# V of the first block in token pairs: loads in runs of 512 bytes, scores in tiles of 64 rows by 32 columns, values in tiles of 32 rows by 64 columns

## The chip, the cores and the metric

The kernel runs on one core of one Trainium2 chip. The metric is the device time of one execution in microseconds (us). The kernel before took 278.22 us, the median of three runs (277.86 to 278.23).

## What is computed

Attention inside chunks of 64 tokens, followed by a feed-forward layer with a squared ReLU. Batch 8, 8 heads, 576 tokens, head dimension 64; the feed-forward layer has 4608 tokens, width 512 and 2048 hidden units.

```python
scores = scale * np.matmul(q_c, k_c.transpose(0, 1, 2, 4, 3))   # per chunk of 64 tokens
attn = np.exp(scores) / np.sum(np.exp(scores), axis=-1, keepdims=True)
out = np.matmul(attn, v_c)
x = out.transpose(0, 2, 1, 3).reshape(B * S, H * D)
h = np.maximum(x @ w_in, 0.0)
return h * h @ w_out
```

## The kernel before

The tokens are worked in nine blocks of 512 (two groups of 256 each). For a block the kernel computes attention, transposes the result `x` to `xT`, multiplies by `w_in` (`ffn_in`, matmuls at line L621, PSUM tiles `ps_ffn`), squares, and multiplies by `w_out` (L795 for the first block, L678 for the others). The order of all instructions is written out by hand, each engine works through its own in that order, and all loads are issued by SyncE's queue (SP), one after another. While PE runs one block's feed-forward layer, attention of the next block is put in between, and loads of later blocks are issued by slot.

The first block has no layer before it to hide behind, and has code of its own, which is what the change touches. It is worked in two halves `u` of four heads, each over 512 tokens (eight chunks):

- `load_half` (L238) loads Q and K of a half, four tokens a partition, so that one run is 1024 bytes. The order on SP is Q, K of half 0, Q, K of half 1, then V of both halves (`load_v_half`, L247, eight loads), then `load_w_in(0)` (L173), all of which are issued ahead of the rest of `w_in`, `w_out` and the loads of block 1.
- `w_in` and `w_out` are loaded in eight pieces of 512 KB each into five buffers `w_st`, and cast to bf16 by GpSimd (POOL, L176 and L184). Two of the 16 hidden tiles `ft` need one piece of `w_in`; the first piece is cast in two halves.
- `transpose_half` (L268, copies L277) transposes Q and K on PE. `keep_busy` (L337) puts matmuls with no use between, to fill PE.
- `scores_half` (L289) multiplies K and Q of each chunk and head on a tile of 64 by 64 of the PE array and takes the exponential `e` on ACT (L296).
- `values_half(e, x, u, j)` (L309) multiplies `e` by V for half of the chunks (`j`) of one half of the heads. V has a column of ones behind each head's 64 columns, so column 64 of the result is the sum of the exponentials. DVE takes its reciprocal (L316) and multiplies (L317). PSUM tiles `ps_att` have two buffers, which scores and values share.
- `transpose_x_half` (L325, copy L329) transposes a quarter of `x` and copies it into `xT`. Four calls make the whole `xT` of the first block.
- V of the first block lies in `v_first`, a view on the space of `w_sum`, so the profile calls it `w_sum`.

At the end of this front the code issues the first half of the contraction of `ft` 0 and 1 (`begun`, four L621 matmuls that need `xT` of heads half 0 alone), and then the whole stream of `ffn_in`.

Of the kernel before, what the change touches and what calls it, by code (L numbers as in the profile page):

```python
# [10 lines left out]
FP32 = mybir.dt.float32  # L11
# [6 lines left out]
def kernel(  # L18
# [9 lines left out]
    nc = tc.nc  # L28

    B, H, S, D = q.shape  # L30
# [49 lines left out]
    w_sum = w_pool.tile([128, 3, n_ft // 2, d_model // 2], BF16, name="w_sum")  # L80
# [57 lines left out]
    for g in range(n_grp):  # L138
        if is_whole(g):
# [3 lines left out]
            b, s = chunks[g][0]  # L143
# [68 lines left out]
    def transpose_qk(g, q_pool, k_pool):  # L212
# [13 lines left out]
            transpose_paired(g, which, bank)  # L226
            copy_paired(copy, qkT[:, which], bank)

    v_first = w_sum.rearrange("p i f c -> p (i f c)")[:, 0:8 * H * (D + 1)].bitcast(
        FP32).rearrange("p (t h d) -> p t h d", t=4, h=H)  # L230
    nc.gpsimd.memset(v_first[:, :, :, D:D + 1], 1.0)

    first = chunks[blocks[0][0]][0]

# [8 lines left out]

    def load_v_half(u):
        b, s = first
        for t in range(4):
            nc.sync.dma_start(  # L247
                out=v_first[:, t, 4 * u:4 * u + 4, 0:D],
                in_=v[b, 4 * u:4 * u + 4, s + 128 * t:s + 128 * t + 128, :].rearrange(
                    "h s d -> s h d"))  # L250

    def bank_bf16():
        return ps_ffn.tile([128, 512], FP32, name="ps_ffn").bitcast(BF16)
# [25 lines left out]
    def scores_half(qkT):  # L279
        qT, kT = (qkT[:, w].rearrange("c t h q -> c (t h q)").rearrange(  # L280
            "c (h n q) -> c h n q", h=2, n=8) for w in range(2))
        ps = ps_att.tile([128, 1024], FP32, name="ps_att")
        for h in range(2):
            for t in range(4):
                for a in range(2):
                    for p in range(2):
                        rows = slice(64 * a, 64 * a + 64)
                        o0 = a * 512 + h * 256 + t * 64
                        nc.tensor.matmul(  # L289
                            out=ps[64 * p:64 * p + 64, o0:o0 + 64],  # L290
                            lhsT=kT[rows, h, 2 * t + p],
                            rhs=qT[rows, h, 2 * t + p],
                            start=True, stop=True)
        e = att_pool.tile([128, 2, n_hp, 2, 64], BF16, name="e")
        flat = e.rearrange("p a h t q -> p (a h t q)")
        nc.scalar.activation(  # L296
            out=flat.rearrange("p (b q i) -> p b q i", q=16, i=4),
            in_=ps.rearrange("p (b i q) -> p b q i", i=4, q=16), func=AF.Exp, scale=scale)
        return flat.rearrange("p (a h t q) -> p a h t q", a=2, h=2, t=4)

    def values_half(e, x, u, j):
        v_bf = v_first.bitcast(BF16)
        ps = ps_att.tile([128, 2, 512], FP32, name="ps_att")
        for t in range(2):
            for h in range(2):
                for a in range(2):
                    for p in range(2):
                        o0 = (2 * t + h) * (D + 1)
                        nc.tensor.matmul(  # L309
                            out=ps[64 * p:64 * p + 64, a, o0:o0 + D + 1],  # L310
                            lhsT=e[64 * p:64 * p + 64, a, h, 2 * j + t, :],
                            rhs=v_bf[64 * p:64 * p + 64, 2 * j + t, 4 * u + 2 * h + a, 1::2],
                            start=True, stop=True)
        o = ps[:, :, 0:4 * (D + 1)].rearrange("p a (h d) -> p a h d", d=D + 1)
        rec = att_pool.tile([128, 2, n_hp], FP32, name="rec", bufs=4)
        nc.vector.reciprocal(out=rec, in_=o[:, :, :, D])  # L316
        nc.vector.tensor_tensor(  # L317
            out=x[:, 4 * j:4 * j + 4].rearrange("p b a d -> p a b d"),
            in0=o[:, :, :, 0:D],
            in1=rec.to_broadcast([128, 2, n_hp, D]),  # L320
            op=ALU.mult)

    def transpose_x_half(x, u, j, copy, psb):
        for b in range(4):
            nc.tensor.transpose(  # L325
                out=psb[:, b * 128:(b + 1) * 128],
                in_=x[:, 4 * j + b].rearrange("p a d -> p (a d)"),
                identity=ident)
        copy(  # L329
            out=xTs[0][:, 2 * j:2 * j + 2, 2 * u:2 * u + 2, :],  # L330
            in_=psb[:, 0:512].rearrange("p (t h q) -> p t h q", t=2, h=2))

    def keep_busy(n, ps=None):
        if ps is None:
            ps = ps_ffn.tile([128, 512], FP32, name="ps_ffn")
        for _ in range(n):
            nc.tensor.matmul(  # L337
                out=ps[:, 0:256], lhsT=ident, rhs=ident_f32.bitcast(BF16), start=True, stop=True)
# [496 lines left out]
    for u in range(2):  # L835
        load_v_half(u)
# [3 lines left out]
    xs = [att_pool.tile([128, 2, n_hp, 2, D], BF16, name="x", bufs=3).rearrange(  # L840
        "p t h a d -> p (t h) a d") for _ in range(2)]
# [4 lines left out]
    transpose_half(kh[0], qkTs[0][:, 1], [V, A], by_token=True)  # L846
    keep_busy(3)
    e0 = scores_half(qkTs[0])
    transpose_half(qh[1], qkTs[1][:, 0], [V])
    keep_busy(2)  # L850
    transpose_half(kh[1], qkTs[1][:, 1], [V, A], by_token=True)
    values_half(e0, xs[0], 0, 0)
    keep_busy(2)
    e1 = scores_half(qkTs[1])
    values_half(e0, xs[0], 0, 1)
    transpose_x_half(xs[0], 0, 0, A, bank_bf16())
    keep_busy(4)
    values_half(e1, xs[1], 1, 0)
    transpose_x_half(xs[0], 0, 1, A, bank_bf16())
    keep_busy(6)  # L860
    xb = [bank_bf16(), bank_bf16()]
    begun = {ft: ps_ffn.tile([128, 512], FP32, name="ps_ffn") for ft in range(2)}
    transpose_x_half(xs[1], 1, 0, A, xb[0])
    values_half(e1, xs[1], 1, 1)
    keep_busy(3, begun[0])
    transpose_x_half(xs[1], 1, 1, V, xb[1])
    for ft in range(2):
# [136 lines left out]
```

## Time and profile before

| | |
|---|---|
| median of three runs | 278.22 us |
| the profiled execution, device time | 277.18 us |
| its span in the profile | 275.4 us, 7355 instructions |
| PE busy | 267.3 us (97%), 3047 matmuls |
| DVE, ACT, POOL busy | 73%, 56%, 34% |
| main DMA queue (q1) | 135968 packets, 55.72 MB, 86.8% of the 16 engines' time |
| DMA queue of instructions (q8) | 24 packets, 0.39 MB |
| granted clock of PE | 1.00 throughout |

The page divides the span into 40 slices of 6.9 us and gives the busy share of each engine in tenths. PE is the engine for matmuls, PEld its weight loads, DVE VectorE, ACT ScalarE, POOL GpSimd, SPq the queue from which SyncE issues DMAs. A line as L621 is a line of the kernel. `out<-in` names the tiles that an instruction writes and reads; what stands in brackets behind a row is the idle time before it and what ended it. The chain of waits is followed back from the last instruction, at each step to what released it.

### The profile page before, as it was taken

How to read it: one execution, taken by the hardware profiler on the slowest of the kernel's cores; microseconds unless marked ns; L12 is line 12 of the kernel's file. 1: busy time of each engine (PE TensorE's matmuls, PEld its weight loads, DVE VectorE, ACT ScalarE, POOL GpSimd, SP SyncE). 2: the span in 40 equal slices, each digit the busy share in tenths (PEclk: the TensorE clock that was granted, in tenths of full speed). 3: DMA queues.
4: the chain of work that ended last, by engine and by line, in shares of the span. 5: the costliest groups of instructions: out<-in, count | busy, mean ns of one | idle time of the engine just before them, and what ended most of it. 6: DMA issues, size and time to landing. Idle time of an engine off the chain costs nothing.

```text
span 275.4 us, 7355 instructions
## 1 busy us (share of the span) xinstructions
PE 267.3 (97%) x3047; PEld 185.5 (67%) x3047; DVE 202.2 (73%) x313; ACT 155.5 (56%) x262; POOL 92.9 (34%) x106
## 2 busy tenths in 40 slices
PE   7889999999999999999999999999999999999994
PEld 4544454888775587658755875587658755875683
DVE  1546516689986997599769776977599769777793
ACT  1537605796347782768186918682768186317710
POOL 2037768140433800380029002900380029003412
PEclk9999999999999999999999999999999999999999
DMA  7999999999999999999999799858799981623004
GB/s 233 228 334 356 369 340 233 227 224 181 286 167 189 261 199 176 292 236 185 259 249 210 153 187 286 189 115 181 225 280 181 210 317 38 193 47 108 0 2 152
DMA packets 136417, 57.11 MB, mean 207 GB/s; under 512 B 110336, under 2 KB 130048, under 8 KB 136384
## 3 DMA queue, kind: packets, MB, share of 16 engines
q1 hardware_dynamic: 135968, 55.72, 86.8%
q0 software_dynamic: 272, 0.79, 0.7%
q8 instruction: 24, 0.39, 0.6%
q10 hardware_dynamic: 144, 0.13, 0.1%
q14 instruction: 9, 0.07, 0.1%
HBM read 36.70 MB, written 9.44 MB: 168 GB/s over the span
## 4 chain that ended last, share of the span: by engine, by line
PE 81%; DMA 9%; SPq 7%; POOL 1%; issue 1%; DVE 0%
PE ps_ffn L678 36%; PE ps_ffn L621 32%; PE ps_ffn L508 8%; DMA w_st<-in_moe_w_in_dram 5%; SPq L247 3%; PE ps_att L420 2%; DMA k_sb<-in_k_dram 2%; DMA w_st<-in_moe_w_out_dram 2%; PE ps_att L392 2%; SPq L162 1%; POOL w_in_bf L176 1%; SPq L158 1%; SPq L238 1%; PE ps_att L447 1%; SPq L181 0%
## 5 line engine op out<-in xcount | busy, mean ns | idle before, releaser
L621 PE MATMUL ps_ffn<-xT,w_in_bf 128*128 128x512 bf16 (+1 forms) x528 | 111.2, 353 | 0.4 <-POOL w_in_bf L176 0.4
L634 POOL TENSOR_TENSOR gT<-rl 128x512 bf16<-128x512 f32 x40 | 45.9, 1162 | 121.1 <-ACT rl L585 120.2
L621 PEld LDWEIGHTS <-w_in_bf 128*128 128x128 bf16 x528 | 50.6, 98 | 37.2 <-POOL w_in_bf L176 1.8
L678 PEld LDWEIGHTS <-w_st 128*128 128x128 bf16 x640 | 62.2, 98 | 7.3
L585 ACT ACTIVATE rl<-ps_ffn 128x512 f32<-128x512 f32 x84 | 50.1, 597 | 29.3 <-PE ps_ffn L621 29.0
L634 DVE TENSOR_TENSOR w_st<-gT 128x2048 bf16<-128x2048 bf16 x40 | 47.4, 1219 | 6.0 <-ACT gT L588 5.9
L678 PE MATMUL ps_ffn<-w_out_bf,w_st 128*128 128x256 bf16 x384 | 45.1, 273 | 0.0
L634 DVE TENSOR_TENSOR gT<-rl 128x512 bf16<-128x512 f32 x30 | 20.8, 693 | 22.6 <-ACT rl L585 22.2
L678 PE MATMUL ps_ffn<-w_sum,w_st 128*128 128x256 bf16 x256 | 29.6, 273 | 0.0
L678 PEld LDWEIGHTS <-gT 128*128 128x128 bf16 x256 | 24.7, 98 | 5.1 <-ACT gT L588 0.6
L612 ACT ACTIVATE rl<-ps_ffn 128x256 bf16<-128x256 f32 (+1 forms) x48 | 20.4, 455 | 6.6 <-PE ps_ffn L621 5.6
L525 DVE SCALAR_TENSOR_TENSOR gT<-rl 128x512 bf16<-128x512 f32 x21 | 23.2, 1103 | 0.4
L616 DVE TENSOR_TENSOR gT<-rl 128x256 bf16<-128x256 bf16 (+1 forms) x41 | 16.2, 438 | 9.6 <-ACT rl L612 9.5
L785 ACT COPY o_sb<-ps_ffn 128x512 f32<-128x512 f32 x7 | 4.1, 587 | 33.6 <-PE ps_ffn L678 33.6
L428 DVE TENSOR_TENSOR x<-ps_att,rec 128x512 bf16<-128x512 f32 x32 | 22.1, 692 | 1.1
L403 ACT ACTIVATE e<-ps_att 128x1024 bf16<-128x1024 f32 x16 | 15.8, 1025 | 4.8 <-PE ps_att L392 4.8
L508 PEld LDWEIGHTS <-w_dif 128*128 128x128 bf16 x140 | 12.9, 98 | 7.1
L678 PE MATMUL ps_ffn<-w_out_bf,gT 128*128 128x256 bf16 x128 | 15.6, 273 | 0.0
L678 PE MATMUL ps_ffn<-w_sum,gT 128*128 128x256 bf16 x128 | 15.3, 273 | 0.0
L176 POOL CAST w_in_bf<-w_st 128x1024 bf16<-128x1024 f32 (+1 forms) x9 | 8.9, 1000 | 17.9 <-DMA w_st<-in_moe_w_in_dram 17.9
L795 PE MATMUL ps_ffn<-w_out_bf,gT 128*128 128x512 bf16 x64 | 14.5, 380 | 0.0
L588 ACT ACTIVATE gT<-rl 128x512 bf16<-128x512 f32 x21 | 13.3, 632 | 0.7
(81 smaller groups left out, 288.8 us busy)
## 6 DMA issues: line engine op xcount, KB each, us to landing
q_sb<-in_q_dram SPq DMA_DIRECT2D x16, 512.0 KB, 6.2
out_dram<-o_sb SPq DMA_DIRECT2D x14, 512.0 KB, 4.6
k_sb<-in_k_dram SPq DMA_DIRECT2D x24, 256.0 KB, 5.9
w_st<-in_moe_w_in_dram SPq DMA_DIRECT2D x8, 512.0 KB, 6.7
w_st<-in_moe_w_out_dram SPq DMA_DIRECT2D x8, 512.0 KB, 6.1
ve_sb<-in_v_dram SPq DMA_DIRECT2D x28, 128.0 KB, 3.7
vo_sb<-in_v_dram SPq DMA_DIRECT2D x21, 128.0 KB, 3.3
k_sb<-in_k_dram SPq DMA_DIRECT2D x4, 512.0 KB, 6.8
```

The lines of the kernel that those rows point to most:

```text
L403: nc.scalar.activation(out=e_out, in_=s_in, func=AF.Exp, scale=scale)
L428: nc.vector.tensor_tensor(out=x[:, t].rearrange("p h a d -> p a h d"), in0=o[:, :, :, 0:D], in1=rec.to_broadcast([128, 2, n_hp, D]), op=AL ...
L508: nc.tensor.matmul(out=out[:, 256 * f:256 * f + 256], lhsT=a[:, d, 128 * f:128 * f + 128], rhs=b[:, :, d, :], start=(first and f == 0 and ...
L525: later.append(lambda: nc.vector.scalar_tensor_tensor(out=place_of(i, jj), in0=both(x), scalar=0.0, in1=both(x), op0=ALU.max, op1=ALU.mult))
L585: nc.scalar.activation(out=rl, in_=h, func=AF.Relu)
L588: nc.scalar.activation(out=gT[:, ft], in_=rl, func=AF.Square)
L612: nc.scalar.activation(out=rl[:, 0:n], in_=h[:, 0:n], func=AF.Relu)
L616: nc.vector.tensor_tensor(out=gT[:, ft, c:c + n], in0=rl[:, 0:n], in1=rl[:, 0:n], op=ALU.mult)
L621: nc.tensor.matmul(out=h[:, 0:n], lhsT=w_in_bf[:, dt, ft * 128:(ft + 1) * 128], rhs=xT[:, c // 128:(c + n) // 128, dt, :], start=(dt == 0) ...
L634: engine.tensor_tensor(out=out, in0=in0, in1=in1, op=op)
L678: nc.tensor.matmul(out=outs[t], lhsT=a[:, i, t * 128:(t + 1) * 128], rhs=b[:, i, :], start=(first and i == 0 and (last or t == 0)), stop=( ...
L795: nc.tensor.matmul(out=o_ps[tt], lhsT=gT[:, ft, tt * 128:(tt + 1) * 128], rhs=w_out_bf[:, ft, :], start=(ft == 0), stop=(ft == n_ft - 1))
```

## The change

V of the first block is loaded with two neighbouring tokens in a partition: four loads, whose runs are 512 bytes, in place of eight with runs of 256. One column of ones serves both tokens of a pair. The keys of a chunk then lie in 32 partitions, even and odd tokens (`i`) apart, so the scores are computed for even and odd keys separately (tiles of 64 rows by 32 columns), and the values are summed over `i` in PSUM from tiles of 32 rows by 64 columns. For even tokens the ones are not beside the 64 columns, so a matmul of one column is made for them: three matmuls (`parts`) for each chunk and head. The bank of the result is now chosen by the pair of chunks `t`, not by the head `a`. Last, the fourth `values_half` is moved ahead, and `keep_busy(6)` becomes `keep_busy(3)` behind it.

```diff
-        for t in range(4):
+        for t in range(2):
             nc.sync.dma_start(
-                out=v_first[:, t, 4 * u:4 * u + 4, 0:D],
-                in_=v[b, 4 * u:4 * u + 4, s + 128 * t:s + 128 * t + 128, :].rearrange(
-                    "h s d -> s h d"))
+                out=v_first[:, t, 4 * u:4 * u + 4, 0:2 * D],
+                in_=v[b, 4 * u:4 * u + 4, s + 256 * t:s + 256 * t + 256, :].rearrange(
+                    "h (s i) d -> s h (i d)", i=2))
...
         for h in range(2):
-            for t in range(4):
-                for a in range(2):
-                    for p in range(2):
-                        rows = slice(64 * a, 64 * a + 64)
-                        o0 = a * 512 + h * 256 + t * 64
-                        nc.tensor.matmul(
-                            out=ps[64 * p:64 * p + 64, o0:o0 + 64],
-                            lhsT=kT[rows, h, 2 * t + p],
-                            rhs=qT[rows, h, 2 * t + p],
-                            start=True, stop=True)
+            for t in range(2):
+                for i in range(2):
+                    for c in range(4):
+                        for a in range(2):
+                            rows = slice(64 * a, 64 * a + 64)
+                            o0 = a * 512 + h * 256 + t * 128 + i * 64
+                            nc.tensor.matmul(
+                                out=ps[32 * c:32 * c + 32, o0:o0 + 64],
+                                lhsT=kT[rows, h, 4 * t + c, i::2],
+                                rhs=qT[rows, h, 4 * t + c],
+                                start=True, stop=True, tile_position=(64 * a, 32 * c))
...
-        for t in range(2):
-            for h in range(2):
-                for a in range(2):
-                    for p in range(2):
-                        o0 = (2 * t + h) * (D + 1)
+        parts = ((0, 0, 0, D), (0, D, 2 * D, 1), (1, 0, D, D + 1))
+        for h in range(2):
+            for a in range(2):
+                for n, (i, lo, at_, m) in enumerate(parts):
+                    for c in range(4):
+                        t, p = divmod(c, 2)
+                        rows = slice(32 * c, 32 * c + 32)
+                        o0 = (2 * h + a) * (D + 1) + lo
+                        vb = v_bf[rows, j, 4 * u + 2 * h + a, 1::2]
                         nc.tensor.matmul(
-                            out=ps[64 * p:64 * p + 64, a, o0:o0 + D + 1],
-                            lhsT=e[64 * p:64 * p + 64, a, h, 2 * j + t, :],
-                            rhs=v_bf[64 * p:64 * p + 64, 2 * j + t, 4 * u + 2 * h + a, 1::2],
-                            start=True, stop=True)
+                            out=ps[64 * p:64 * p + 64, t, o0:o0 + m],
+                            lhsT=e[rows, a, h, j, i, :],
+                            rhs=vb[:, at_:at_ + m],
+                            start=(h == a == n == 0), stop=(i == 1),
+                            skip_group_check=True, tile_position=(32 * c, 64 * p))
...
     values_half(e1, xs[1], 1, 0)
     transpose_x_half(xs[0], 0, 1, A, bank_bf16())
-    keep_busy(6)
+    values_half(e1, xs[1], 1, 1)
+    keep_busy(3)
     xb = [bank_bf16(), bank_bf16()]
     begun = {ft: ps_ffn.tile([128, 512], FP32, name="ps_ffn") for ft in range(2)}
     transpose_x_half(xs[1], 1, 0, A, xb[0])
-    values_half(e1, xs[1], 1, 1)
     keep_busy(3, begun[0])
```

More of the change, by code (lines that the diff above doesn't have):

```diff
@@ L227, in transpose_qk @@
             copy_paired(copy, qkT[:, which], bank)
-    v_first = w_sum.rearrange("p i f c -> p (i f c)")[:, 0:8 * H * (D + 1)].bitcast(
-        FP32).rearrange("p (t h d) -> p t h d", t=4, h=H)
-    nc.gpsimd.memset(v_first[:, :, :, D:D + 1], 1.0)
+    VE = 2 * D + 1
+    v_first = w_sum.rearrange("p i f c -> p (i f c)")[:, 0:4 * H * VE].bitcast(
+        FP32).rearrange("p (t h e) -> p t h e", t=2, h=H)
+    nc.gpsimd.memset(v_first[:, :, :, 2 * D:VE], 1.0)
     first = chunks[blocks[0][0]][0]
@@ L298, in scores_half @@
             in_=ps.rearrange("p (b i q) -> p b q i", i=4, q=16), func=AF.Exp, scale=scale)
-        return flat.rearrange("p (a h t q) -> p a h t q", a=2, h=2, t=4)
+        return flat.rearrange("p (a h t i q) -> p a h t i q", a=2, h=2, t=2, i=2)
     def values_half(e, x, u, j):
@@ L303, in values_half @@
         ps = ps_att.tile([128, 2, 512], FP32, name="ps_att")
-        for t in range(2):
-            for h in range(2):
-                for a in range(2):
-                    for p in range(2):
-                        o0 = (2 * t + h) * (D + 1)
-                        nc.tensor.matmul(
-                            out=ps[64 * p:64 * p + 64, a, o0:o0 + D + 1],
-                            lhsT=e[64 * p:64 * p + 64, a, h, 2 * j + t, :],
-                            rhs=v_bf[64 * p:64 * p + 64, 2 * j + t, 4 * u + 2 * h + a, 1::2],
-                            start=True, stop=True)
-        o = ps[:, :, 0:4 * (D + 1)].rearrange("p a (h d) -> p a h d", d=D + 1)
+        parts = ((0, 0, 0, D), (0, D, 2 * D, 1), (1, 0, D, D + 1))
[7 more added lines that the diff above has]
+                        vb = v_bf[rows, j, 4 * u + 2 * h + a, 1::2]
+                        nc.tensor.matmul(
+                            out=ps[64 * p:64 * p + 64, t, o0:o0 + m],
[3 more added lines that the diff above has]
+                            skip_group_check=True, tile_position=(32 * c, 64 * p))
+        o = ps[:, :, 0:4 * (D + 1)].rearrange("p t (b d) -> p t b d", d=D + 1)
         rec = att_pool.tile([128, 2, n_hp], FP32, name="rec", bufs=4)
@@ L317, in values_half @@
         nc.vector.tensor_tensor(
-            out=x[:, 4 * j:4 * j + 4].rearrange("p b a d -> p a b d"),
+            out=x[:, 4 * j:4 * j + 4].rearrange("p (t b) a d -> p t (b a) d", t=2),
             in0=o[:, :, :, 0:D],
```

## The prediction

> **What bounds the kernel now.** I read the page's rows of busy tenths first, then the chain of waits in order of time, then the timeline and the table by stage for the first 20 us, and last the waits of the DMA queue's issues. The page says that TensorE (PE) is full from the third slice of 6.9 us on, and that the DMA engines are full from the second to slice 20.
>
> ```profile
> PE   7889999999999999999999999999999999999994
> ...
> DMA  7999999999999999999999799858799981623004
> ```
>
> The stages make it exact. The columns are: stretch, its length, busy time of PE, PEld, DVE, ACT and POOL with counts, granted clock, DMA share, GB/s.
>
> ```profile
> 0.00:18.00 18.00, 13.72 (x244) 9.23 (x245) 6.79 (x13) 6.27 (x8) 2.39 (x26) 1.00 0.90 250
> 18.00:48.00 30.00, 30.00 (x226) 13.64 (x225) 13.88 (x20) 14.78 (x25) 22.86 (x21) 1.00 1.08 329
> 48.00:50.00 2.00, 1.92 (x44) 1.54 (x43) 1.42 (x3) 0.71 (x2) 0.33 (x1) 1.00 1.27 210
> 50.00:268.00 218.00, 217.98 (x2508) 157.99 (x2506) 177.29 (x272) 133.36 (x227) 64.90 (x56) 1.00 0.87 189
> ```
>
> After 18 us PE has no idle time worth the name, so the end moves by as much as the start of the feed-forward stream moves, if its feeds move too. That start is the first L621 matmul. The chain of waits up to it runs through the SP queue and the first weights (columns: start, length, what):
>
> ```profile
> 12.28 0.51 SPq L173
> ...
> 12.83 5.73 DMA w_st<-in_moe_w_in_dram
> ...
> 18.62 1.05 POOL w_in_bf L176
> ```
>
> The eight V loads (L247) hold SP from 2.88 to 12.24 us; only then is `w_in` issued. Beside that runs the attention front on PE and DVE (start, length, engine, line):
>
> ```profile
> 12.33 0.75 PE L309 MATMUL ps_att<-w_sum,e 64*64 64x65 bf16 x16 [0.32 <-DVE x L317]
> ...
> 13.78 0.45 PE L309 MATMUL ps_att<-w_sum,e 64*64 64x65 bf16 x16
> ...
> 15.59 0.45 PE L309 MATMUL ps_att<-w_sum,e 64*64 64x65 bf16 x16
> ...
> 16.33 0.69 DVE L317 TENSOR_TENSOR x<-ps_att,rec 128x512 bf16<-128x512 f32 x1
> ...
> 17.07 0.40 PE L325 MATMUL ps_ffn<-ident,x 128*128 128x128 bf16 x4 [0.60 <-DVE x L317]
> 17.22 1.17 POOL L176 CAST w_in_bf<-w_st 128x512 bf16<-128x512 f32 x2 [14.94 <-DMA w_st<-in_moe_w_in_dram]
> 17.51 0.42 DVE L329 COPY xT<-ps_ffn 128x512 bf16<-128x512 bf16 x1 [0.49 <-PE ps_ffn L325]
> 17.88 0.11 PEld L621 LDWEIGHTS <-w_in_bf 128*128 128x128 bf16 x2 [0.59 <-POOL w_in_bf L176]
> 17.89 14.29 PE L621 MATMUL ps_ffn<-xT,w_in_bf 128*128 128x512 bf16 x64 [0.41 <-POOL w_in_bf L176]
> ```
>
> Two paths meet at 17.9: the weights (cast from 17.22, released by the landing at 17.17) end last, and attention has its four last transposes issued at about 17.3. Inside the stream the starts are 0.216 us apart but for two waits on casts, 0.12 us at 18.45 and 0.17 us at 21.65, so the stream behaves as if it began at **18.17**. The second wait belongs to the third `w_in` load (landed 20.49, cast until 21.59, wanted 16 matmuls or 3.45 us after the start: 18.14).
>
> **The change, part by part.** *V loads: 8 of 128 KB in 256 B runs become 4 of 256 KB in 512 B runs.* Each still has 512 runs, so an issue costs what it costs now: the first four take from 2.88 to 8.29 us, and `w_in` is issued at 8.33, not 12.28. It then follows V without a hole; today the DMA share is 0.80 at 11 to 12 us and 0.57 at 12 to 13. V's transfer: today the second K lands at 9.76 and the last V load at 14.87, 5.1 us. Around 45 to 47 us the queue carries 512 B runs at 304 to 323 GB/s, so 1.05 MB takes 3.4 us. One `w_in` load is 1.50 us (landings 20.49, 22.01, 23.52). The first would land at 9.76 + 3.4 + 1.5 = 14.66 (now 17.17), the third at 17.66.
>
> *Instruction blocks.* The page's 24 packets of its instruction queue are 16 KB each. The first begins at 9.98 us, after 216 executed PE instructions, the second at 18.34, after 495. It takes 1.3 us of one DMA engine, and the V load that was under way then landed 1.18 us after the one before it, where its neighbours came 0.59 apart: 0.6 us later, and what follows keeps the lag. The change adds 378 PE instructions, all ahead of the stream (64 more pairs of weight load and matmul in the scores, 128 in the values, 3 `keep_busy` pairs fewer), so blocks fall due at about 8.5, 12 and 14.3 us. I charge 0.5 us each: V's first load lands at 9.76 + 0.85 + 0.5 = 11.1, the third `w_in` at 17.66 + 1.5 = 19.2. Between none and 0.6 each, that landing is 17.7 to 19.5. It moves from 20.49 by 1.3, so the weights allow a start at 18.14 − 1.3 = **16.85** (15.3 to 17.1). [...]
>
> *Scores: 32 matmuls on 64x64 tiles become 64 on 64 rows by 32 columns.* Today's 32 weight loads of one call take 0.33 us, 10.5 ns each, with four tiles in flight. With eight, the price lies between the same total (0.33) and the same rate (0.67); I take 0.5. Of the two calls the first hides behind the landing of K at 9.76, for which PE waited 0.61 us; the second comes after the first values. No trace shows 32-column tiles, so both ends stay. Weights taken with a stride of two elements are seen already (L268).
>
> *Values: 16 matmuls become 48, on tiles of 32 rows by 64 columns.* Today two tiles are in flight and 16 loads take 0.34 us, 21 ns each. In the new form four are in flight, as in the scores row, so I take that rate: 48 x 10.5 = 0.5 us, +0.16 a call; at the values' own rate it is 1.0, +0.67 a call. A price below today's is excluded: there are three times the instructions on at most twice the tiles. The 16 one-column matmuls in each call are charged as full ones. [...]
>
> *Order.* The last `values_half` moves ahead of the `keep_busy` and of the transposes of the third `x`. It is queued behind no new wait: its PSUM buffer is free once `x` of the call two before it is written. Three fillers go; PE waits there for DVE anyway. The V memset halves from 0.15 us on an idle POOL, nothing. Activation, reciprocal and multiply keep their sizes (1.02, 0.21, 0.69).
>
> *The attention path summed.* First values 11.1 to 11.75 (today's second half started at 10.99 and ended at 11.31). DVE takes 0.95, so `x` is written at 12.75 (12.28). Second values 12.8 to 13.45 (12.33 to 13.08). The second scores and their exponentials lie beside this. Third values, after transposes and fillers, 14.15 to 14.8 (13.78 to 14.23). Fourth values directly behind, until 15.55 (16.04). DVE is now the serial part: two rounds of reciprocal and multiply, 0.93 each, from 14.85 to 16.7 (17.02). Transposes at 16.75; four of them, 0.2 us; the stream can begin at **17.0**. The copy into `xT` ends at 17.6, needed by the fifth matmul, 0.86 after the start. With cheap values and no lag of V this is 16.3; with +0.67 a call it is 18.25.
>
> *Sum.* The later path, 17.0, against 18.17: 1.17 us, taken as 1.2. The profiled execution took 277.18 (its span of 275.4 and 1.8 around it): 276.0. The median of the runs, 278.22, is 1.04 above the profiled one; off it the forecast is **277.0**. Cover: loads after this move with the queue, which is full until 48 us; their landings move by the 1.3 of the weights, no less than PE does. If they did not, the second K of block 1 (landed 49.15, used at 49.20) would be late next.
>
> **The rivals.**
> 1. *Weights still end last.* The blocks cost more than the 0.6 us seen, or V's pitch of 516 B in SBUF slows its runs. For: DMA is full from 2 us on. Against: `w_in` is queued 3.95 us sooner. At 0.75 us for each block the third load lands at 19.9, the weights allow 17.6, and the gain is 0.6: 277.6.
> 2. *Row tiles of one bank take turns.* Two of the four row groups write one bank (`t`), in different partitions; if a bank takes one at a time, 16 full pairs of 42 ns (two tiles at 21 ns each today) and 8 short ones of half that make 0.84 us a call, +0.34 over my charge; three calls lie on the path: +1.0, gain 0.2, 278.0. Against it: today's pair of L309 matmuls on rows 0 to 63 and 64 to 127 writes one bank too, and starts 3 ns apart at 13.78. [...]
> 3. *Slower: tiles of 32 do not overlap at all.* 48 pairs of 42 ns are 2.0 us a call, +1.5 over mine, three times on the path, and 64 in the second scores add more than 2: the start comes near 23, some 5 us late, 283. It decides from about 0.9 us a values call on. For: no such tile is in the trace. Against: tiles of 64 overlap in both directions.
> 4. *Given back at 49 us.* The loads of block 1 do not come earlier, PE starts sooner and waits there: 278.2. For: the chain's step `42.96 6.20 DMA k_sb<-in_k_dram` ends 0.05 before PE. Against: one queue in order, full since 14 us.
>
> **How the numbers follow.** Forecast 0.60 (276.2 to 277.6 alone), rival 1 0.12, rival 2 0.09, rival 3 0.09, rival 4 0.10. About 0.2% (0.56 us) is what a measurement of this kernel can tell from no change. Faster is the forecast and rival 1: 0.72; same is rivals 2 and 4: 0.19; slower is rival 3: 0.09. The range takes all but rival 3: from cheap values and unlagged V (gain 1.9, and the runs' own spread of 0.3) to no change and 0.2 above it: 276.0 to 278.4.
>
> **What would show it.** Right: four L248 issues end near 8.3; the first `w_in` lands at 14.7 to 15.8; values calls of 0.4 to 0.6 us of loads; first L621 near 17.0 and no waits behind it; PE gapless at 49 us. Wrong: values calls of a microsecond or more (rivals 2, 3), a first L621 that waits for a POOL cast (1), PE waiting for `k_sb` (4). The forecast falls if the stream starts later than 17.6.

## The result, and the profile after

| | before | after |
|---|---|---|
| median | 278.09 us (277.86 to 278.23, 4 runs) | 285.89 us (283.97 to 286.85, 4 runs) |
| after / before | | 1.0273, 95% interval 1.0209 to 1.0336 |
| the profiled execution, its span | 277.18, 275.4 us | 283.97, 282.2 us |
| PE and PEld instructions ahead of the stream | 486 | 864 |
| granted clock over the span | 1.00 | 0.988 |

The change makes the kernel 2.7% slower: 7.8 us by the medians, 6.8 by the profiled executions. The page of the kernel after, the 40 slices of 7.06 us:

```profile
PE   7739999999989999999999999999999999999995
...
PEclk9968999999999999999999999999999999999999
DMA  6999999889998927999999789986999982514003
```

PE is at 3 tenths in the third slice, where it was at 8 before, and the granted clock falls there, which it did nowhere before. The table by stage of the kernel after (stretch, length, busy time and count of PE, PEld, DVE, ACT and POOL, granted clock, DMA share, GB/s):

```profile
8.00:12.60 4.60, 2.98 (x163) 2.18 (x141) 1.64 (x4) 1.61 (x2) 0.00 (x0) 1.00 1.15 319
12.60:16.70 4.10, 2.28 (x152) 1.77 (x150) 1.54 (x3) 1.50 (x2) 0.97 (x2) 1.00 1.07 343
16.70:23.60 6.90, 3.81 (x83) 3.08 (x83) 1.80 (x4) 1.17 (x2) 4.60 (x6) 0.51 1.10 350
23.60:31.60 8.00, 8.00 (x40) 3.61 (x39) 4.49 (x7) 5.17 (x9) 6.57 (x6) 1.00 1.02 362
```

PE and PEld start 255 instructions in the 4.1 us of the second row (its counts hold those still running from before, too), all of them by 14.97, and 166 in the 6.9 of the third, at half the clock. The timeline of PE (start, length, instruction; in brackets the idle time before it and what ended it):

```profile
11.67 0.58 PE L315 MATMUL ps_att<-w_sum,e 32*64 32x64 bf16 x48 [0.23 <-DMA w_sum<-in_v_dram]
...
12.51 0.29 PE L291 MATMUL ps_att<-qkT 64*32 64x64 bf16 x25
13.04 0.47 PE L291 MATMUL ps_att<-qkT 64*32 64x64 bf16 x39 [0.24 <-issue]
...
14.71 0.42 PE L315 MATMUL ps_att<-w_sum,e 32*64 32x64 bf16 x32
19.80 0.44 PE L315 MATMUL ps_att<-w_sum,e 32*64 32x65 bf16 x16 [4.67 <-issue]
...
20.70 0.86 PE L315 MATMUL ps_att<-w_sum,e 32*64 32x64 bf16 x48
...
23.59 4.70 PE L628 MATMUL ps_ffn<-xT,w_in_bf 128*128 128x512 bf16 x21
```

Two thirds through the third `values_half`, between matmuls 32 and 33 of the same 48, PE stops for 4.67 us. The releaser is "issue": PE waited for nothing that the profile shows as an event, no semaphore, no data, no other engine. The stream starts at 23.59 and nothing waits behind it; before, it behaved as if begun at 18.17. The chain of waits has the same hole:

```profile
14.78 0.35 PE ps_att L315 x25
15.13 4.67 issue
19.80 0.44 PE ps_att L315 x11
```

Where does it come from? The instruction queue of the DMA engines (q8) answers it. Its rows in the DMA view (packets, MB, share of 16 engines), from 17.2 to 19.8 us:

```profile
q1 hardware_dynamic: 905, 0.90, 106.5%
q8 instruction: 1, 0.02, 2.7%
```

The same view for 12.6 to 17.2 us has no row of q8 at all. By the packets' own records, the block of instructions that PE lacks starts to move at 17.30 and PE goes on at 19.80, 2.5 us later. The small stop at 13.04 answers in the same way to the packet of 10.43. Counted from the first PE instruction, loads and matmuls together, PE stops at number 447 and at number 701, 254 apart (256 with the two semaphore instructions of PE that the trace has between them); the page's 25 packets of 0.41 MB are 16 KB each, one more than before, for 378 more PE instructions. That made the theory that the experiments test.

### The profile page after: what moved, and what is told of

The parts are those of the page before. It is cut to its first block, busy times and chain, and to the rows that moved or that the text cites. A ratio compares the mean times of both kernels' runs of the same rounds, so it can differ in the third digit from the quotient of the medians.

```text
span 282.2 us, 7727 instructions
## 1 busy us (share of the span) xinstructions
PE 268.4 (95%) x3236; PEld 187.1 (66%) x3236; DVE 204.1 (72%) x313; ACT 155.2 (55%) x262; POOL 93.2 (33%) x106
## 4 chain that ended last, share of the span: by engine, by line
PE 88%; DVE 4%; DMA 3%; issue 3%; SPq 1%; ACT 1%; DVEq 0%
PE ps_ffn L628 35%; PE ps_ffn L685 32%; PE ps_ffn L515 8%; PE ps_ffn L802 5%; DMA w_sum<-in_v_dram 3%; DVE w_st L641 2%; PE ps_att L427 2%; PE ps_att L399 2%; DVE x L435 1%; PE ps_att L315 1%; PE ps_ffn L344 1%; SPq L239 1%; PE ps_att L454 1%; PE ps_ffn L332 1%; PE ps_att L201 1%
## 5 line engine op out<-in xcount | busy, mean ns | idle before, releaser
L592 ACT ACTIVATE rl<-ps_ffn 128x512 f32<-128x512 f32 x84 | 50.1, 596 | 29.3 <-PE ps_ffn L628 29.1
L641 DVE TENSOR_TENSOR w_st<-gT 128x2048 bf16<-128x2048 bf16 x40 | 49.4, 1271 | 6.0 <-ACT gT L595 5.9
L623 DVE TENSOR_TENSOR gT<-rl 128x256 bf16<-128x256 bf16 (+1 forms) x41 | 17.5, 471 | 7.5 <-ACT rl L619 7.0
L410 ACT ACTIVATE e<-ps_att 128x1024 bf16<-128x1024 f32 x16 | 15.8, 1024 | 4.8 <-PE ps_att L399 4.8
L685 PE MATMUL ps_ffn<-w_out_bf,gT 128*128 128x256 bf16 x128 | 15.6, 273 | 0.0
L176 POOL CAST w_in_bf<-w_st 128x1024 bf16<-128x1024 f32 (+1 forms) x9 | 8.6, 964 | 16.7 <-DMA w_st<-in_moe_w_in_dram 16.7
```

The source lines that it names most:

```text
L410: nc.scalar.activation(out=e_out, in_=s_in, func=AF.Exp, scale=scale)
L592: nc.scalar.activation(out=rl, in_=h, func=AF.Relu)
L623: nc.vector.tensor_tensor(out=gT[:, ft, c:c + n], in0=rl[:, 0:n], in1=rl[:, 0:n], op=ALU.mult)
L641: engine.tensor_tensor(out=out, in0=in0, in1=in1, op=op)
L685: nc.tensor.matmul(out=outs[t], lhsT=a[:, i, t * 128:(t + 1) * 128], rhs=b[:, i, :], start=(first and i == 0 and (last or t == 0)), stop=( ...
```

## The experiments

**Theory 1, supply:** PE's instructions come in blocks (the stops are 254 apart), the packet of a block starts only once PE is in the block before it (in the kernel after 446 is passed at 13.04, the packet starts at 17.30), and the new front uses them up faster than the DMA engines bring them. What counts is the number of instructions, whatever they compute. **Theory 2, tiles:** the 32-row or 32-column tiles, or their accumulation in one bank, stop PE. **Theory 3, loads:** the loads of V, or `w_in` moved close behind them, hold something up.

This table collects what the traces showed. "Ahead" is the number of PE and PEld instructions that start ahead of the stream. A stop is given by the time from the last start before it to the next one; the last number before it is 445 to 447, and 700 or 701. "Clock 0.5" is the stretch of the first 30 us in which the granted clock was 0.5. The time is a median, but a single run for b_rep_values, b_rep_scores, a_two, a_hold, a_hold_long and b_dma_look.

| kernel | ahead | stop near 446 | stop near 700 | q8 packets start | clock 0.5 | stream | us |
|---|---|---|---|---|---|---|---|
| before | 486 | none | not in the front | 9.98, 18.34 | never | 17.89 | 278.09 |
| after | 864 | 12.60 to 13.04 | 14.97 to 19.80 | 10.43, 17.30 | 16.7 to 23.6 | 23.59 | 285.89 |
| b_repeat | 870 | 11.74 to 12.86 | 17.07 to 19.03 | 10.12, 16.56 | 12.3 to 29.3 | 24.75 | 287.37 |
| b_rep_values | 742 | 12.81 to 13.19 | 17.30 to 19.01 | 10.47, 16.74 | 18.6 to 25.4 | 21.03 | 282.88 |
| b_rep_scores | 614 | 12.19 to 13.38 | not in the front | 10.70, 17.57 | 13.1 to 19.9 | 20.23 | 278.82 |
| a_two | 736 | 11.70 to 13.70 | 17.45 to 20.52 | 11.01, 17.93 | 12.4 to 26.1 | 22.83 | 286.75 |
| a_two_lean | 684 | 11.06 to 14.52 | not in the front | 11.80, 19.00 | 12.2 to 22.5 | 19.46 | 280.45 |
| a_hold | 864 | 11.53 to 13.61 | 16.68 to 20.46 | 11.09, 17.28 | 12.2 to 25.8 | 24.27 | 285.7 |
| a_hold_long | 864 | 11.51 to 14.38 | 17.45 to 18.21 | 12.00, 15.74 | 14.4 to 28.1 | 25.08 | 288.0 |
| b_order | 480 | none | not in the front | 10.5, 18.54 | never | 16.93 | 277.79 |
| b_dma_look | 486 | none | not in the front | 12.35, 19.07 | not in the front | 16.70 | 279.56 |
| b_dma_order | 480 | 14.15 to 14.62 | not in the front | 11.94, 18.78 | never | 16.30 | 276.86 |
| hybrid | 608 | none (a wait for V) | not in the front | 10.87, 18.42 | never | 17.20 | 277.39 |

**b_repeat: the kernel before with as many instructions as the change.** Old loads, old order, old tiles; each matmul of the first block's scores is followed by a one-column repeat of itself, each of the values by two. Its three fillers more make 870 instructions where the change has 864.

```diff
+for m in (64, 1):                       # scores
+    nc.tensor.matmul(out=ps[64 * p:64 * p + 64, o0:o0 + m], lhsT=..., rhs=qT[rows, h, 2 * t + p, 0:m], ...)
+for lo in (0, D, D):                    # values
+    nc.tensor.matmul(out=ps[64 * p:64 * p + 64, a, o0 + lo:o0 + D + 1], lhsT=..., rhs=vb[:, lo:D + 1], ...)
```

> The kernel before, with its old V loads and its old 64x64 tiles; each score matmul of the first block is issued a second time for one column and each values matmul a second and third time for the column of ones. So the front has 64 + 128 more pairs of weight load and matmul, the same number as the change adds, and nothing else of the change. Theory 1 (PE runs out of instructions: they come in blocks of 256, and a block is used up in about 2 us there while the next takes 5 to 7): a stop of 4 to 5 us after some 705 executed PE instructions, in the third call of the values, as in the changed kernel; granted clock at half for several us behind it; 283 to 287 us. Theory 2 (tiles of 32 rows or columns stop the array): no stop, 278 to 279. Theory 3 (the earlier transfers of w_in stand in the way of V or of e, a wait that the profile does not name): no stop, 278 to 279.

Measured: 287.37 us, 1.0249 times the kernel before on the same chip (1.015 to 1.0348). PE's timeline there:

```profile
12.87 0.71 PE L290 MATMUL ps_att<-qkT 64*64 64x1 bf16 x36 [0.93 <-issue]
...
19.03 0.64 PE L312 MATMUL ps_att<-w_sum,e 64*64 64x1 bf16 x16 [1.77 <-issue]
```

The whole loss is there with no small tile, no new load and no new order. It stops at number 446 and number 700 again, here in the scores and in the second half of the third values. Neither theory 2 nor theory 3 can produce this.

**b_rep_scores and b_rep_values: one of the two repeats each.**

> The kernel before with only the scores' matmuls issued twice: 64 pairs more, about 618 PE instructions ahead of the feed-forward stream in place of 490. Theory 1: the 705th instruction lies in the stream, where 87 instructions last 9 us, so the next block is there in time: no stop, within 0.5 us of the kernel before (278.0 to 278.6). Theories 2 and 3: the same; it is the lower point of the dose.

> The kernel before with only the values' matmuls issued three times: 128 pairs more, about 746 PE instructions ahead of the stream. Theory 1: the 705th comes at the end of the front, near 16.5 us, so the stop is there but later in the program (fourth call of the values or the last transposes), shorter by what was done before it: 2 to 4 us, 280 to 283. Theories 2 and 3: no stop, 278 to 279.5.

Measured, one run each beside a kernel before of 278.95: 278.82 and 282.88. With 742 instructions ahead there is a stop at 700, in yet another place, the fourth values:

```profile
19.01 0.59 PE L311 MATMUL ps_att<-w_sum,e 64*64 64x1 bf16 x14 [1.55 <-issue]
```

With 614 number 700 falls into the stream, where matmuls are 0.216 us apart at full clock, and there is none. I had expected no stop at all there; PE stopped for 1.01 us idle at 446, because the second block was reached at 12.2, only 1.5 us after its packet had started. So it is not a fixed number of instructions that is allowed, but a race between PE and each block. Its stream starts 2.3 us later than in the profile of before, and yet its time is not longer; one run can't settle that, since the kernel before took 276.85 to 279.82 us on this chip.

**b_dma and b_dma_look: the new loads alone.** V is loaded in pairs of tokens as in the change; the code that computes is the one of before. Its values multiply other numbers than V's, so only its time is read.

```diff
+rhs=v_bf[64 * p:64 * p + 64, j, 4 * u + 2 * h + a, 1::2][:, t * D:t * D + D + 1],   # plus the change's v_first and load_v_half
```

> The kernel before with the new V loads alone (four of 256 KB in runs of 512 bytes); scores and values keep their tiles, order and number of matmuls, and the values read 65 columns of the new tile that are not V's, so only the time is read. Theory 1 with the prediction's sum for the loads: w_in lands about 1.3 to 1.8 us earlier, no stop, and the start of the stream is then set by the attention path in its old order at 17.3 at the earliest: 277.2 to 277.8. Theory 2: the same. Theory 3 (the loads are what hurts): a stop or a late front, 280 or more.

> The new V loads alone once more, for a profile (the values multiply numbers that are not V's, so only the time is read): the first w_in lands at 14.7 to 15.8, no stop of PE, the first matmul of the stream at 17.0 to 17.6.

Measured: b_dma 276.78, ratio 0.9952 (0.9914 to 0.9989), a little more gain than expected. One execution, the profiled one, took 1293.48 us, its stream matmuls 1.70 us long on average (the first nine) where those of before take 0.38; no run shows why, it is not in the ratio, and its trace says nothing of the front. The loads by themselves are a gain, so theory 3 is out as the cause of the loss. b_dma_look, a single run, took 279.56: stream at 16.70 (17.0 to 17.6 expected), no stop in the front, and a new idle time of PE of 1.97 us up to 72.14, of which below.

The loads do have a part in when a block comes. With the old tiles and the new loads the first q8 packet starts at 12.35 and 11.94 (b_dma_look, b_dma_order), with the old loads at 9.98 and 10.5 (before, b_order).

**a_two: the values in two matmuls instead of three.** With a column of ones on either side of the pair, even and odd tokens take 65 neighbouring columns each, and DVE adds the two sums. The tiles stay 32 by 64; 128 instructions fewer.

```diff
-parts = ((0, 0, 0, D), (0, D, 2 * D, 1), (1, 0, D, D + 1))
+for i in range(2):
 ...
+    out=ps[64 * p:64 * p + 64, t, o0:o0 + D + 1], rhs=vb[:, i * (D + 1):(i + 1) * (D + 1)]
 ...
+nc.vector.reduce_sum(out=rec, in_=o[:, :, :, 0:DE:DE - 1], axis=mybir.AxisListType.X)
```

> The changed kernel with a second column of ones, one on either side of a head's pair of tokens: each chunk and head then takes two matmuls of 65 columns and no matmul of one column, and DVE adds the two sums (one more small DVE operation of about 0.2 us a call). 64 pairs of weight load and matmul fewer in the front: about 736 PE instructions ahead of the stream, of which the 701st lies at the end of the fourth call of the values. Theory 1 (blocks of 256 PE instructions that come too late): the stop stays, at the same 701st instruction, so in another call of the values, and PE resumes near 19.5 as before, with less left to do: the stream at 21 to 22.5, 281 to 284. Theory 2 (something in the third call itself, its tiles or operands, stops PE): the stop stays in the third call, at its 33rd load: 284 to 287.

Measured: 286.75 us (one run, before 278.02), outside what theory 1 had led me to expect and inside the range of theory 2. The place decides between them, and it came as theory 1 has it, number 700, now after 28 of the 32 matmuls of the fourth values:

```profile
17.09 0.60 PE L315 MATMUL ps_att<-w_sum,e 32*64 32x65 bf16 x28
20.52 0.27 PE L315 MATMUL ps_att<-w_sum,e 32*64 32x65 bf16 x4 [2.83 <-issue]
```

In the time the first stop counts too: number 446 now cost 2.0 us, its packet coming 0.6 us later than in the kernel after, and the clock was at half from 12.4 to 26.1.

**a_two_lean: a_two with fewer fillers.** `keep_busy(12)` becomes six fillers of 512 columns, and the later `keep_busy` calls go.

> As the kernel with two columns of ones, and the fillers cut: the first twelve become six of 512 columns, the other twenty are left out. About 684 PE instructions ahead of the stream, so that the 701st is some ten matmuls inside it. Theory 1: a stop of at most 1 us in the stream, which starts near 17: 277 to 279, unless PE without fillers falls to half clock, which adds 1 to 3 us. Theory 2: the stop stays in the third call of the values: 283 to 287.

Measured: 280.45 us, 1.0084 (1.0046 to 1.0122). Number 700 lies in the stream and nothing stops there, but without fillers PE comes to 446 even sooner, at 11.06, and sits for longer (3.27 us, the row `14.53 0.25 PE L291` of its timeline), with the clock at half from 12.2 to 22.5. So here the fillers had also given the next block time to come.

**b_order: the new order alone** (the fourth `values_half` ahead, three fillers fewer).

> The kernel before with the new order alone (the fourth call of the values ahead, three fillers fewer); loads, tiles and number of matmuls stay. By the prediction's sum the stream starts when w_in allows it (18.17), and only the attention path, which has time to spare, gets shorter: no change, 277.9 to 278.4, ratio 0.999 to 1.001. Rival: attention sets the start already, then it gains up to 0.5 us.

Measured: 277.79 us, 1.0002 (0.996 to 1.0043), as expected. In its profile attention ends sooner and PE waits for the weights instead:

```profile
16.93 9.30 PE L621 MATMUL ps_ffn<-xT,w_in_bf 128*128 128x512 bf16 x41 [0.30 <-POOL w_in_bf L176]
```

The start at 16.93 is not the order's alone. With the same eight V loads, SP issued `w_in` at 10.67 in this execution and at 12.28 in that of before, and the first cast started at 16.26 and not at 17.22: single profiles differ by about a microsecond here.

**a_hold and a_hold_long: the kernel after, with `w_in` kept back.** If the block of instructions waits behind the data in the DMA engines, it must come sooner where they are empty. A small copy on SP that reads `x` holds `load_w_in(0)` until the first values are done, or until the third.

```diff
-load_w_in(0, n_cast=2)
 ...
+held = const_pool.tile([128, 32], BF16, name="held")
+nc.sync.dma_start(out=held, in_=xs[0][:, 3, 0, 0:32])   # a_hold_long: behind the third values, xs[1]
+load_w_in(0, n_cast=2)
```

> The changed kernel with the loads of w_in held back on SP until the first quarter of x is written (a small copy inside SBUF that reads x is put ahead of them), so that from about 12.5 to 14 us the DMA engines have only the tail of V. It asks why the block takes so long: it was due at about 12.8 us and its packet began at 17.3. If it queues behind the data that is already issued: the packet begins by 14.5 to 15, PE resumes by 17.5, the stop is 2 us or less in place of 4.7, and w_in lands near 17 as in the kernel before: 279 to 281. If the delay is the block's own, whatever else the engines carry: the packet begins near 17 again, the stop is 4 to 5 us, 283 to 287.

> The changed kernel with the loads of w_in held back on SP until the first quarter of the second x is written, which comes behind the third call of the values; so from the landing of V (about 14 us) to the stop's end the DMA engines carry no data at all. It settles what the shorter hold left open. If a block of instructions queues behind data: the second packet begins within 2.5 us of PE's crossing (so by 15.5 to 16), PE resumes by 18. If the delay is the block's own: the packet begins 3.4 to 4.5 us behind the crossing, near 17.3, and PE resumes near 20, as in all kernels with w_in behind V. The time is long in both (w_in is late): 283 to 290.

a_hold, 285.7 us, decides nothing by itself. Its packet started at 17.28, as I had expected of a delay of the block's own, but SP issued `w_in` from 12.81 on, and PE went on past 446, behind which the second packet starts in every run of the table, at 13.61, so `w_in` was in the queues again. a_hold_long, 288.0 us, does. SP issues nothing until 19.66, as its row shows, and the DMA view of 15.0 to 16.4 us there has this packet alone:

```profile
19.66 0.56 SPq L866 DMA_DIRECT2D held<-x  x1
```

```profile
DMA packets 1, 0.02 MB, mean 12 GB/s; under 512 B 0, under 2 KB 0, under 8 KB 0
...
q8 instruction: 1, 0.02, 4.8%
```

PE goes on past 446 at 14.38, the packet starts at 15.74, 1.36 us later, and the stop at 700 is nearly gone, where the kernel after had 4.67 and a_hold 3.60:

```profile
18.21 0.43 PE L315 MATMUL ps_att<-w_sum,e 32*64 32x65 bf16 x16 [0.58 <-issue]
...
25.08 1.46 PE L628 MATMUL ps_ffn<-xT,w_in_bf 128*128 128x512 bf16 x3 [2.85 <-POOL w_in_bf L176]
```

The time is worse since the weights are late, as the second row says, and the first stop and the half clock are still there; the run was for the stop alone. In the kernel after the same step took from 13.04 to 17.30, 4.26 us. The stops themselves compare fairly only with a_hold: there as here the half clock was on, and PE took 3.07 us from 446 to 700, where the kernel after took 1.93 and so had longer to wait. From the crossing to the first instruction of the block a_hold needs 6.85 us (13.61 to 20.46), the kernel after 6.76, a_hold_long 3.83 (14.38 to 18.21). So the DMA engines' load accounts for about 3 us of a stop, most of it, by one run; the 3.83 us remain with empty engines.

**b_dma_order: new loads and new order, old tiles,** 480 instructions ahead (values of other numbers again).

> The new V loads and the new order together, with the old tiles and the old number of matmuls (the values multiply numbers that are not V's, so only the time is read). It is the change without its added instructions. By the prediction's sum the weights allow 16.85 and the attention path 16.7 to 17.0, so the stream starts near 17.0 and the time is about 1.2 us under the kernel before: ratio 0.994 to 0.998, and no stop of PE. If the prediction's gain was wrong by itself, not only overtaken by the stop: ratio 1.0 or more.

Measured: 276.86 us, 0.9941 (0.9915 to 0.9966), 1.6 us less than before by the ratio, 1.3 by the medians. I had expected no stop; there is a small one at 446. PE's timeline:

```profile
14.62 0.25 PE L310 MATMUL ps_att<-w_sum,e 64*64 64x65 bf16 x4 [0.28 <-issue]
...
16.30 4.05 PE L622 MATMUL ps_ffn<-xT,w_in_bf 128*128 128x512 bf16 x17
```

The stream starts at 16.30 without a wait behind it. The profiled execution is this kernel's slowest (278.45; the runs go from 275.59), and shows where part of the gain can be lost: PE is idle for 0.34 and 1.62 us, up to 69.08 and 72.12, ahead of the scores of a later block (L393). This is the view of that line, what its engine waited for (us, times; the waits of PE and of PEld are added up):

```profile
  DMA qkT<-qkb: 4.5, 4
```

SP's two transposing DMAs took longer than before, here the rows of the two kernels' SP timelines, first before, then b_dma_order:

```profile
62.68 4.17 SPq L363 DMA_TRANSPOSE qkT<-qkb  x2
```

```profile
63.28 6.71 SPq L364 DMA_TRANSPOSE qkT<-qkb  x2
```

Why they take longer in some executions was not tested.

**hybrid: the two gains, fewer instructions, V's own numbers.** Half 0 of the heads as before, half 1 in pairs with the two-matmul values of a_two, and the new order: six loads of V and 608 instructions ahead.

```diff
 e0 = scores_half(...)                    # half 0 unchanged, four loads
+if u: for t in range(2): nc.sync.dma_start(out=v_pairs[:, t, :, 1:2 * D + 1], ...)
+e1 = scores_pairs(qkTs[1])
+values_pairs(e1, xs[1], 1, 0)
+values_pairs(e1, xs[1], 1, 1)
+keep_busy(3)
```

> Half of the change: V of the first four heads is loaded and multiplied as before, V of the other four in pairs of tokens with a column of ones on either side (two matmuls a chunk and head), and the new order. About 608 PE instructions ahead of the stream. The 446th comes at the start of the third call of the values, near 13.9 us, when its block is there or nearly so; the 701st lies ten us inside the stream. Theory 1: no stop but perhaps 0.5 us at the 446th; half of the loads' gain stays, 0.3 to 0.8 us: ratio 0.997 to 0.999, faster than both kernels. If small tiles or half-sized loads cost something of their own: 1.002 or more.

Measured: 277.39 us, 0.9966 (0.9934 to 0.9997): faster than before by about 0.9 us, by an interval that only just leaves out 1, and than the change by 8.5. The stream starts at 17.20 with no stop at a block and full clock, so the small tiles by themselves bring no stop:

```profile
14.21 0.46 PE L369 MATMUL ps_att<-w_sum,e 32*64 32x65 bf16 x32 [1.09 <-DMA w_sum<-in_v_dram]
14.61 0.40 PE L387 MATMUL ps_ffn<-ident,x 128*128 128x128 bf16 x4
14.93 0.46 PE L369 MATMUL ps_att<-w_sum,e 32*64 32x65 bf16 x32
...
17.20 9.11 PE L683 MATMUL ps_ffn<-xT,w_in_bf 128*128 128x512 bf16 x41
```

Its PE waits 1.09 us for V near 446; that wait gave the block time. Its packet started at 10.87, and in the runs that stopped at 446 PE went on 2.4 to 2.7 us after the packet's start.

## Why the prediction was wrong

**The step that failed is "Instruction blocks".** It found the blocks and, after 216 and 495 PE instructions, their first two packets in the trace of before, and reckoned how many more there would be. Then it charged a block as a transfer that delays other transfers, 0.5 us each on V and `w_in`, and never asked whether PE would have its instructions in time. It took the blocks as moving when due, at 8.5, 12 and 14.3 us, an estimate that no run shows; their packets started at 10.43, 17.30 and 22.07. The rows of before allowed the question: the block of 9.98 was not used before number 446, at 15.6, so its lateness was free. With the change number 446 is reached at 12.60 and number 700 at 14.97. In place of that term the trace of after has 0.24 us and 4.67 us of idle PE, and a half clock from 16.7 to 23.6.

Against the forecast start at 17.0 the 6.6 us up to 23.59 are: the third values at 14.71, not 14.15, +0.56 (V 0.5 later, and the first stop); the second stop, +4.67; and the rest, 1.36, the work from the stop to the stream at half clock (it took 3.79 us; the forecast has 2.4 from the same point, and the fourth values' row shows 0.86 where the second took 0.58). A last 1.4 us came later: from 23.59 to the end of the span are 258.6 us, before they were 257.2 from 18.17. PE waits for `x` of the next block near 62, 81 and 82 us (0.44, 0.60 and 0.51 us, of which two rows of the timeline follow), which it did nowhere before. Why DVE was late there, I did not follow. 276.0 + 6.6 + 1.4 is 284.0, the profiled execution took 283.97.

```profile
81.23 0.22 PE L427 MATMUL ps_att<-ve_sb,e 64*64 64x65 bf16 x2 [0.60 <-DVE x L435]
...
82.07 0.22 PE L427 MATMUL ps_att<-ve_sb,e 64*64 64x65 bf16 x2 [0.51 <-DVE x L435]
```

**V loads.** The step held, but without its charge for blocks. The rows of SP's queue and of POOL in the timeline of after:

```profile
2.87 6.38 SPq L248 DMA_DIRECT2D w_sum<-in_v_dram  x4
9.30 10.82 SPq L173 DMA_DIRECT2D w_st<-in_moe_w_in_dram  x8
15.73 1.17 POOL L176 CAST w_in_bf<-w_st 128x512 bf16<-128x512 f32 x2 [13.48 <-DMA w_st<-in_moe_w_in_dram]
```

`w_in` is issued at 9.30 (forecast 8.33, before 12.28), the first V lands at 11.63 (11.1), and the first cast starts at 15.73, right behind a landing that was forecast for 14.7 to 15.8. The third load of `w_in` lands at 18.63 (forecast 19.2, before 20.49); the run without the added instructions has it at 18.59 (b_dma_order). The second K landed at 10.76, 1.0 later than in the profile of before, and from there to the third `w_in` are 7.87 us, where the forecast has 7.90 without any charge for blocks and 9.4 with it. So no price of the blocks on these transfers is seen; why K was late was not followed.

**Scores and values.** Both prices were about right. PE's weight loads of after (shape, count):

```profile
7.77 0.57 PEld L291 LDWEIGHTS <-qkT 64*32 64x32 bf16 x64 [0.41 <-DVE qkT L278]
...
13.44 0.46 PEld L315 LDWEIGHTS <-e 32*64 32x64 bf16 x48
```

0.57 us for a call of scores and 0.46 for one of values, where 0.5 each was taken, both at full clock. The rival that lets tiles of one bank take turns needed 0.84 a values call, and the slower rival, in which tiles of 32 do not overlap, 2.0; both fall with this row. The slower rival's 283 us is close to the measured time, but for another reason.

**Order and sum.** Without the added instructions the forecast gain is borne out: b_dma_order has the stream at 16.30 (17.0) and is 1.6 us faster by the ratio (1.2). Weights last (rival 1) is what b_order alone shows, 0.30 us; with the new loads it is gone. Giving back later was seen, but not as rival 4 has it: at 70 us and not 49, behind the transposes of `qkT` and not the loads of `k_sb`. Three details of the prediction are off and decide nothing: +0.67 a call is 0.51 over the charge, and three such calls on the path, as rival 2 counts them, give 18.5 and not 18.25; and in the busy rows of before PE is full from the fourth slice, not the third, and the DMA engines up to the 22nd, not the 20th.

**How far ahead the blocks came.** The packet of the block behind number 701 started only after PE had passed 446 (13.04, then 17.30), so in this run PE had no more than one block ahead of the one it was in.

## What to carry to other kernels

Before cutting matmuls into smaller tiles, count PE's instructions and compare the time that a block of them takes (254 here) with the time of a block's arrival: PE used one up in 1.9 us, and one needed 3.8 us with the DMA engines empty and 6.8 us with them full of loads. An idle time put down to "issue", at the same instruction number to within two whatever the code, that ends 2.3 to 3.2 us after a q8 packet has started, was this shortage in every run here. Fewer PE instructions in the same stretch cured it (hybrid); fewer fillers alone made PE wait sooner and longer (a_two_lean). To tell it from the tiles' own price, repeat the old instructions until their number is that of the new code.

## What the runs showed of the hardware that was not expected

- **The next block came later with data in the queues.** From the moment PE enters a block to the start of the next packet: 4.26 us with `w_in` in the queues (after; 2.7 in before to 4.5 in a_two_lean over the other runs), 1.36 with empty DMA engines (a_hold_long). From the packet's start to PE's next instruction another 2.3 to 2.7, once 3.2.
- **Half a clock came with the stops.** In each run whose front stopped for 0.9 us or more at a block the granted clock was then 0.5 for a while: 16.7 to 23.6 in the kernel after, 12.3 to 29.3 in b_repeat. By the table it lasted 6.8 or 6.9 us in three runs, 10.3 in one, 13.6 or 13.7 in three and 17.0 in b_repeat. But a wait of 1.09 us in hybrid left the clock at 1.0, and stops of 0.93 and 1.01 did not (b_repeat, b_rep_scores), and in b_repeat the clock fell 0.3 us after PE had gone idle. So how much idle time it takes, and how much of it was the stop's, is not settled here.
- **Row tiles that write one bank cost no more for it.** 48 loads of 32 by 64 in 0.46 us, on four tiles with two row tiles to a bank, in different partitions, are 9.6 ns each, no dearer than the 64 by 64 scores of before (10.5).
